# Attention and SiLU MLP on one core: batches 4 to 7 through seven products after the last scores, PSUM as one tile of named banks, exponentials of four banks, first scores on all strips

## The chip, the cores and the metric

The kernel runs on one core of one Trainium2 chip. The metric is the device time of one execution in microseconds, as a median over runs. Engines are named as in the profile: PE multiplies matrices (PEld loads its weights), DVE and ACT are the vector and scalar engines, POOL issues most loads, SP issues the stores. Matmul results go to PSUM, a memory of eight banks of 512 float32 columns on 128 partitions.

## What is computed

Eight batches, twelve heads, 448 tokens, 64 numbers per head; then an MLP over the 3584 tokens, 768 to 2048 to 768, with SiLU.

```python
def _attn_ref(q, k, v):
    scores = np.matmul(q, k.transpose(0, 1, 3, 2)) / np.sqrt(q.shape[-1])
    attn = np.exp(scores - np.max(scores, axis=-1, keepdims=True))
    attn = attn / (np.sum(attn, axis=-1, keepdims=True) + 1e-09)
    return np.matmul(attn, v)
def _moe_ref(x, w_in, w_out):          # x: the heads of a token side by side
    h = x @ w_in
    return (h / (1.0 + np.exp(-h))) @ w_out
```

The output is float32; the kernel gets q, k, v and the weights in the 16-bit type that the profile shows (f16).

## The kernel before, in words

**Attention.** A unit is one batch and a group of four heads (`hg`, three per batch). Batch 0 is cut into two pieces of 224 tokens (`PIECES`), so it has six units; later batches have three. The scores of a unit come in bursts of matmuls (L325): each of four heads lies on its own strip of 32 partitions of PE, and matmuls on different strips run side by side. A burst fills up to four PSUM banks, in two tiles "s" of two banks; `expo` (L357, its instruction L362) reads one tile, 128x896, into E. DVE adds E tiles for the row sums (L373), PE multiplies E by V (L388) and sums (L404), DVE forms the reciprocal of the sums (`inverse`, L447 sT, L455, L461 rdn) and writes the normalized x as xT (`norm`, L477).

For the units below `HALVES` (6: all of batch 0) a burst holds only two of the four heads, one "s" tile at a time, so only two strips work; later units score four heads in one burst.

**First matmul.** `ffn1` (L491): six matmuls of 448 columns (224 for batch 0) per block f of 128 of the 2048 columns. ACT takes the tanh into `th` (L502), DVE forms the gated value in G (`gate`, L536; SiLU as (tanh + 1) times h, with halved inputs). Batches 6 and 7 go by seven products instead (Strassen's scheme in Winograd's form, halves of the tokens being the two batches): `combine_x` and `combine_w_in` (L601, tw) form sums on DVE, `pair_product` (L625, "f") makes 7 x 3 matmuls per f of eight, five adds on DVE (L656), two copies (L650) and four SiLU (L663) on ACT finish them.

**Second matmul.** A pair of batches has seven tiles of 128 tokens; two consecutive tiles form a quad, which goes by seven products of eight matmuls of 384 columns each (`combine_g` L686, `product` L696, "p"); the first quad is plain (L710, "o"). DVE and ACT read the results (L750, L754, L757), `store` (L745) issues output DMAs on SP, at the very end on ACT too.

**What sets the order.** A planner in Python (`Order`, `Ring`, `Op`) runs ahead of the emission. It keeps a clock for each engine, estimated costs (`act(n)`, `mm(n)`), and rings that stand for buffers: "s" 2 tiles, "m" 4 single banks for everything else in PSUM, E 9 tiles, V 2 whole batches, xT 6. Whenever PE is free it picks a score burst (L1291 `run_qk`; between bursts of later batches at least `PACE`, 2.6 us by its clock), an attention step (`run_av`), or the next work of the MLP (`moe_ready`, L1235). The result is one list of instructions, sorted by planned time; each engine runs its part of it in order. One `ffn1` of six matmuls is one step for the planner, so a score burst stands between such steps.

Before the first h (batch 0's first `ffn1`) there is nothing to fill PE's waits, so `run_zeros` (L1455, matmuls L1459) puts matmuls of 128 zero columns there, in a bank of their own taken from the "m" ring.

Of the kernel before, what the change touches and what calls it, by code (L numbers as in the profile page):

```python
# [29 lines left out]
def act(n):  # L30
    return n * 0.00087 + 0.13


class Ring:


    def __init__(self, n):
        self.free = [0.0] * n

    def can(self, n, now):  # L40
        return len(self.free) >= n and heapq.nsmallest(n, self.free)[-1] <= now

    def when(self, n):
        return heapq.nsmallest(n, self.free)[-1] if len(self.free) >= n else None

    def take(self, n=1):
        for _ in range(n):
            heapq.heappop(self.free)

    def give(self, at):  # L50
        heapq.heappush(self.free, at)
# [25 lines left out]

class Order:


    def __init__(self, shy):
        self.now, self.shy = 0.0, shy
        self.free = {"PE": 1.0, "ACT": 2.1, "DVE": 1.2, "POOL": 1.2}
        self.wait = {"ACT": [], "DVE": []}
        self.pool = []
        self.dma_free = 0.0
        self.out = []
        self.mode = None
        self.busy = {e: 0.0 for e in self.free}
# [16 lines left out]
    def on_pe(self, op, mode):  # L106
        gap = SWITCH if mode != self.mode else 0.0
        self.mode = mode
        op.busy += gap
        self.start(op)  # L110

# [54 lines left out]
def kernel(  # L166
# [32 lines left out]
    EAGER = 1  # L199
    HALVES = 6  # L200
    NEAR, LATE = 0.15, -2.0
    COLD, FIRST = 8.5, 47
    SHY = 0.5
    TWB, SXB = 4, 4
    PIECES = ((0, 7), (7, TPP))
    NE, NX3, NT_ = 9, 6, 2
# [29 lines left out]

    rawk, rawq, KT, QT, VT, E, T, acc, rdn_t, xT, g_t, ost_t = ({} for _ in range(12))
# [24 lines left out]
    def load_v(b, hg0, hg1, x):  # L262
        if b not in VT:
            VT[b] = sb.tile([128, NH, NCH, D], FP16, name=f"V_{b}", tag="V", bufs=2)
        hs = slice(HG * hg0, HG * hg1)
        first, count = X_TOK[form(b, hg0)][x]
        nc.gpsimd.dma_start(  # L267
            out=VT[b][32 * x : 32 * (x + 1), hs, 0:count, :],
            in_=v[b, hs].rearrange("h (i g) d -> i h g d", g=TPP)[
                :, :, first : first + count, :  # L270
            ],
        )
# [42 lines left out]
    def score_banks(n, w, ys):  # L315
        for y in ys:
            pS_t[(n, w, y)] = ps.tile(
                [128, 2, 512], FP32, name=f"s_{n}_{w}_{y}", tag="s", bufs=2
            )

    def score(pS, n, c, e, h, x0, x1, p0):
# [8 lines left out]
            stop=(e == 1),  # L330
        )
# [5 lines left out]
    def scores(n, w, ys):  # L337
        score_banks(n, w, ys)
# [7 lines left out]
    def scores_rest(n):  # L346
        score_banks(n, 3, (0, 1))
# [9 lines left out]
    def expo(n, w, y):  # L357
        kr = rows_of(n, w * per_burst(n))
        nk = 32 * (units[n][3] - units[n][2]) * per_burst(n)
        if (n, w) not in E:  # L360
            E[(n, w)] = sb.tile([128, HG, S], FP16, name=f"E_{n}_{w}", tag="E", bufs=NE)
        nc.scalar.activation(  # L362
            out=E[(n, w)][0:kr, 2 * y : 2 * y + 2, 0:nk],
            in_=pS_t[(n, w, y)][0:kr, :, 0:nk],
# [15 lines left out]
    def attend_mm(a, n, part, c, h, k0, k1, e, start, stop):  # L380
# [5 lines left out]
        else:  # L386
            w = VT[b][k0:k1, HG * hg + h, c, part - 1 :: 2]
# [5 lines left out]
            stop=stop,  # L393
        )

    def attend_sums(ns):
        a = ps.tile([128, 512], FP32, name=f"a_{ns[0]}_0", tag="m", bufs=4)
        for n in ns:
            acc[(n, 0)] = a
        for i, (w, e) in enumerate(  # L400
            ((half[0], T[ns[0]]), (half[1], T[ns[1]]), (both, E[(ns[0], 3)]))
        ):
            for h in range(HG):
# [5 lines left out]
                    stop=(i == 2),  # L409
                )  # L410

    def attend(ns, part):
# [4 lines left out]
        for n in ns:  # L417
            acc[(n, part)] = ps.tile([128, 512], FP32, name=f"a_{n}_{part}", tag="m", bufs=4)

# [22 lines left out]
    def inverse(ns, step, i=0):  # L442
        g0, g1 = units[ns[0]][2:]
        shape = [128, g1 - g0, 32]
        if step == 0:
            sT_t[ns[0]] = sb.tile(shape, FP32, name=f"sT_{ns[0]}", tag="sT", bufs=1)
# [11 lines left out]
        else:  # L458
            n = ns[i]
            rdn_t[n] = sb.tile(shape, FP32, name=f"rdn_{n}", tag="rdn", bufs=2)  # L460
            nc.vector.transpose(  # L461
                out=rdn_t[n], in_=inv_t[ns[0]][:, :, i : i + 1].to_broadcast(shape)
            )

    def x3(b, cc):
        if (b, cc // 3) not in xT:
            xT[(b, cc // 3)] = sb.tile(
                [128, 3, S], FP16, name=f"xT_{b}_{cc // 3}", tag="xT", bufs=NX3
            )
        return xT[(b, cc // 3)]  # L470

    def norm(n, part):
# [3 lines left out]
        x3(b, cc)  # L476
        nc.vector.scalar_tensor_tensor(  # L477
            out=x3(b, cc)[:, cc % 3, 32 * g0 : 32 * g1],
# [7 lines left out]
    h_t, th_t, o_t = {}, {}, {}  # L486

    def ffn1(b, f, t0, t1):
        h = ps.tile([128, 512], FP32, name=f"h_{b}_{f}_{t0}", tag="m", bufs=4)
        for cc in range(NDC):  # L490
            nc.tensor.matmul(  # L491
                out=h[:, 0 : t1 - t0],
                lhsT=w_in_t[:, cc, 128 * f : 128 * (f + 1)],
                rhs=x3(b, cc)[:, cc % 3, t0:t1],
                start=(cc == 0),
                stop=(cc == NDC - 1),
            )
        h_t[(b, f, t0)] = h

    def tanh(b, f, t0, t1):  # L500
        th = sb.tile([128, t1 - t0], FP16, name=f"th_{b}_{f}_{t0}", tag="th", bufs=3)
        nc.scalar.activation(out=th, in_=h_t[(b, f, t0)][:, 0 : t1 - t0], func=AF.Tanh)  # L502
        th_t[(b, f, t0)] = th

# [3 lines left out]
    X = const.tile([128, NFF, 128], FP16, name="X")  # L511
# [18 lines left out]
    def gate(b, f, t0, t1):  # L530
        r = b % 2
        cut = 6 * 128 - S if b % 4 == 1 else S
        for lo, hi, dst, at in ((0, cut, G, S * r), (cut, S, X, -cut)):
            lo, hi = max(lo, t0), min(hi, t1)
            if lo < hi:
                nc.vector.scalar_tensor_tensor(  # L536
                    out=dst[:, f, at + lo : at + hi],
                    in0=th_t[(b, f, t0)][:, lo - t0 : hi - t0],
                    scalar=1.0,
                    in1=h_t[(b, f, t0)][:, lo - t0 : hi - t0],  # L540
                    op0=ALU.add,
                    op1=ALU.mult,
                )

    def rows(t, i):
# [3 lines left out]
        if u % 2 == 0 and k == NT - 1:  # L549
            return X[:, fs]  # L550
# [4 lines left out]
    PB = B - 2  # L555
    c_t, sx_t, tw_t, pp_t, pf_t = {}, {}, {}, {}, {}

    def old_buffer(name, home, cols):

        if home == "V":  # L560
            t = sb.tile([128, NH, NCH, D], FP16, name=name, tag="V", bufs=2)
            t = t.rearrange("p h c d -> p (h c d)")
        else:
            t = sb.tile([128, HG, S], FP16, name=name, tag="E", bufs=NE)
            t = t.rearrange("p h s -> p (h s)")
        return [
            t[:, 3 * cols * i : 3 * cols * (i + 1)].rearrange("p (c t) -> p c t", c=3)
            for i in range(2 if home == "V" else 1)
        ]

    def combine_x(m):
        if m < 4:
            made = old_buffer(f"sx_{m}", "V" if m == 3 else "E", S)
            for i, t in enumerate(made):
                sx_t[m + i] = t
        x = {(r, i): x3(PB + r, 3 * i) for r in range(2) for i in range(2)}
        a, b, op = {
            1: (x[1, 0], x[1, 1], ALU.add),
            2: (sx_t.get(1), x[0, 0], ALU.subtract),
            3: (x[0, 0], x[1, 0], ALU.subtract),  # L580
            4: (x[0, 1], sx_t.get(2), ALU.subtract),
        }[m]
        nc.vector.tensor_tensor(out=sx_t[m], in0=a, in1=b, op=op)
# [5 lines left out]
    def combine_w_in(m, f0):  # L589
        if (m, f0) not in tw_t:  # L590
            made = old_buffer(f"tw_{m}_{f0}", W_HOME.get((m, f0), "E"), 512)
            for i, t in enumerate(made):
                tw_t[(m + i, f0)] = t
# [9 lines left out]
    W_HOME = {(1, 0): "V"}  # L603
    PBANK = {1: "A", 2: "A", 6: "B", 5: "C", 3: "C", 7: "D", 4: "D"}

    def pair_product(f, m):
        if m in (1, 5):
            pp_t[(f, PBANK[m])] = ps.tile(
                [128, 512], FP32, name=f"f_{f}_{m}", tag="m", bufs=4
            )[:, 0:S]  # L610
        elif m == 6:
            two = ps.tile([128, 2, 512], FP32, name=f"f_{f}_{m}", tag="s", bufs=2)
            pp_t[(f, "B")], pp_t[(f, "D")] = two[:, 0, 0:S], two[:, 1, 0:S]
        x = {(r, i): x3(PB + r, 3 * i) for r in range(2) for i in range(2)}
        lo, at = f // 4 * 4, slice(128 * (f % 4), 128 * (f % 4 + 1))
        a, w = {
            1: (x[0, 0], w_in_part(0, 0, f, f + 1)),
            2: (x[0, 1], w_in_part(1, 0, f, f + 1)),
            3: (sx_t.get(4), w_in_part(1, 1, f, f + 1)),
        }.get(m, (None, None))  # L620
        if a is None:
            i = {4: 4, 5: 1, 6: 2, 7: 3}[m]
            a, w = x[1, 1] if m == 4 else sx_t[i], tw_t[(i, lo)][:, :, at]
        for c in range(3):
            nc.tensor.matmul(  # L625
                out=pp_t[(f, PBANK[m])],
                lhsT=w[:, c, :],
                rhs=a[:, c, :],
                start=(c == 0 and m in (1, 6, 5, 7)),
                stop=(c == 2),  # L630
                skip_group_check=True,
            )

    def pair_tmp(f, name):
        tag, n, shape, dt = {
            "p": ("rq", NRQ, [128, TPP * D], FP16),
            "q": ("rk", NRK, [128, TPP * D], FP16),
# [914 lines left out]
```

## Time and profile of the kernel before

| What | Value |
|---|---|
| median of 3 runs | 393.91 us (393.77 to 394.09) |
| span of the profiled execution | 393.02 us |
| median less that span | 0.89 us |
| granted PE clock | 1.00 in the windows from 30 us on |
| first h (L491) starts | 30.23 us |
| zeros L1459 | 87 matmuls |
| scores L325, all forms | 864 matmuls |
| h L491 | 192 of 224 columns, 480 of 448 |
| pair product f L625 | 168 of 448 columns |
| second matmul p L696 and o L710 | 728 and 64 of 384 columns |
| exponentials | 156 of 128x896, 16 of 96x896 |
| tanh L502 | 32 of 224, 80 of 448 columns |

The profile's time is of one execution, and its zero is the start of the span; the median is taken over the runs, outside of the profiler's span. "Busy" counts an engine's instructions; in the groups, the number behind the bar is the total busy time, then the mean time of one in ns, then the engine's idle time ahead of that group and what ended it. Consecutive matmuls overlap, so the time from start to start (the spacing) is less than the mean of one. The chain of work that ended last lists, step by step, what stood on the path to the end.

### The profile page before, as it was taken

What the parts mean: (1) busy time and instruction counts of PE and PEld (TensorE: products, weight loads), DVE (VectorE), ACT (ScalarE), POOL (GpSimd) and SP (SyncE); (2) the same over time, 40 slices, a digit from 0 to 9 for tenths busy, and PEclk for the clock granted to TensorE, in tenths of its full rate; (3) what the DMA queues carried; (4) which work ended last, traced back from release to release, by engine and by line L of the source; (5) the groups of instructions that cost most, each with busy time, mean ns of one, the idle gap of its engine ahead of it and who ended that gap; (6) DMA issues with size and microseconds to landing.
All of it is one profiled execution on the core that took longest, in us unless ns stands there. A gap on an engine that the chain in (4) does not pass through costs nothing.

```text
span 393.0 us, 9255 instructions
## 1 busy us (share of the span) xinstructions
PE 386.6 (98%) x3679; PEld 199.7 (51%) x3679; DVE 296.2 (75%) x610; ACT 238.7 (61%) x365; POOL 83.7 (21%) x153
## 2 busy tenths in 40 slices
PE   8999999999999999999999999999999999999996
PEld 7667774444444434454444444444444555555663
DVE  2476676999988696895968967876879897777652
ACT  4988885696855869626778258575693218772000
POOL 6632455406006060600063116000000000000000
PEclk9999999999999999999999999999999999999999
DMA  7999999919047573753183567202000140001443
GB/s 112 205 210 210 161 166 179 182 37 141 2 82 115 109 103 39 121 99 86 25 116 48 102 125 115 38 2 61 21 3 2 46 100 17 2 1 37 97 98 93
DMA packets 35579, 34.43 MB, mean 88 GB/s; under 512 B 11600, under 2 KB 34000, under 8 KB 35536
## 3 DMA queue, kind: packets, MB, share of 16 engines
q0 software_dynamic: 24784, 22.82, 39.2%
q1 hardware_dynamic: 9984, 10.24, 10.2%
q10 hardware_dynamic: 768, 0.79, 0.8%
q8 instruction: 29, 0.48, 0.5%
q14 instruction: 14, 0.11, 0.1%
HBM read 45.61 MB, written 11.01 MB: 144 GB/s over the span
## 4 chain that ended last, share of the span: by engine, by line
PE 94%; DMA 2%; DVE 1%; ACT 1%; issue 0%; POOL 0%; SPq 0%; ACTq 0%; DVEq 0%; POOLq 0%
PE p L696 29%; PE h L491 29%; PE s L325 12%; PE a L388 10%; PE f L625 8%; PE o L710 3%; PE a L404 2%; DMA rk<-in_k_dram 2%; DMA out_dram<-ost 1%; PE z L1459 1%; DVE tw L601 0%; ACT E L362 0%; DVE ost L750 0%; SPq L745 0%; DVE KT L302 0%
## 5 line engine op out<-in xcount | busy, mean ns | idle before, releaser
L362 ACT ACTIVATE E<-s 128x896 f16<-128x896 f32 (+1 forms) x172 | 150.0, 915 | 44.9 <-PE s L325 43.6
L491 PE MATMUL h<-xT,w_in_t 128*128 128x448 f16 (+1 forms) x672 | 118.2, 326 | 0.0
L491 PEld LDWEIGHTS <-w_in_t 128*128 128x128 f16 x672 | 61.5, 98 | 54.4 <-issue 17.7
L502 ACT ACTIVATE th<-h 128x448 f16<-128x448 f32 (+1 forms) x112 | 54.3, 494 | 33.6 <-PE h L491 24.9
L536 DVE SCALAR_TENSOR_TENSOR G<-th,h 128x448 f16<-128x448 f16 (+2 forms) x112 | 55.4, 508 | 16.5 <-ACT th L502 14.7
L267 POOL DMA_DIRECT2D V<-in_v_dram x88 | 48.6, 568 | 50.2 <-PE a L388 35.7
L325 PE MATMUL s<-rq,KT 32*128 32x448 f16 (+4 forms) x864 | 56.7, 340 | 0.8 <-ACT E L362 0.4
L696 PEld LDWEIGHTS <-G 128*128 128x128 f16 x384 | 36.3, 98 | 28.5 <-issue 4.8
L696 PEld LDWEIGHTS <-S 128*128 128x128 f16 x312 | 29.5, 98 | 23.8 <-issue 3.4
L388 PE MATMUL a<-E,V 128*32 128x448 f16 (+3 forms) x864 | 39.9, 334 | 0.0
L696 PE MATMUL p<-w_out_t,S 128*128 128x384 f16 x208 | 38.1, 326 | 0.5 <-DVE xT L477 0.5
L696 PE MATMUL p<-D,G 128*128 128x384 f16 x208 | 38.1, 326 | 0.0
L252 POOL DMA_DIRECT2D rq<-in_q_dram x27 | 15.1, 560 | 104.7 <-PE s L325 88.7
L750 DVE TENSOR_TENSOR ost<-p,u 128x384 f32<-128x384 f32 x39 | 21.6, 555 | 19.4 <-PE p L696 15.5
L477 DVE SCALAR_TENSOR_TENSOR xT<-a,rdn 128x448 f16<-128x448 f32 (+1 forms) x54 | 28.6, 565 | 7.0 <-PE a L388 6.2
L325 PEld LDWEIGHTS <-KT 32*128 32x128 f16 (+2 forms) x864 | 17.5, 98 | 28.9 <-issue 26.0
L696 PE MATMUL p<-w_out_t,G 128*128 128x384 f16 x176 | 31.9, 326 | 0.0
L373 DVE TENSOR_TENSOR T<-T,E 128x1792 f16<-128x1792 f16 x20 | 21.7, 1087 | 10.2 <-ACT E L362 10.2
L388 PEld LDWEIGHTS <-V 128*32 128x32 f16 (+2 forms) x864 | 17.8, 95 | 20.8 <-issue 13.5
L373 DVE TENSOR_TENSOR T<-E,E 128x1792 f16<-128x1792 f16 x20 | 21.6, 1082 | 5.5 <-ACT E L362 5.5
L757 ACT COPY ost<-p 128x384 f32<-128x384 f32 x13 | 6.2, 480 | 32.0 <-PE p L696 21.1
L302 DVE STREAM_TRANSPOSE KT<-rk 128x256 f32<-128x256 f32 (+3 forms) x48 | 16.7, 386 | 6.8 <-DMA rk<-in_k_dram 6.8
(70 smaller groups left out, 344.5 us busy)
## 6 DMA issues: line engine op xcount, KB each, us to landing
out_dram<-ost SPq DMA_DIRECT2D x208, 48.0 KB, 1.6
rk<-in_k_dram POOLq DMA_DIRECT2D x24, 224.0 KB, 5.0
rq<-in_q_dram POOLq DMA_DIRECT2D x21, 224.0 KB, 5.4
w_in_t<-in_moe_w_in_dram POOLq DMA_DIRECT2D x6, 512.0 KB, 11.4
w_out_t<-in_moe_w_out_dram POOLq DMA_DIRECT2D x4, 768.0 KB, 13.6
V<-in_v_dram POOLq DMA_DIRECT2D x43, 64.0 KB, 4.0
V<-in_v_dram POOLq DMA_DIRECT2D x40, 48.0 KB, 3.9
out_dram<-ost ACTq DMA_DIRECT2D x16, 48.0 KB, 1.8
```

The source lines that it names most:

```text
L267: nc.gpsimd.dma_start(out=VT[b][32 * x : 32 * (x + 1), hs, 0:count, :], in_=v[b, hs].rearrange("h (i g) d -> i h g d", g=TPP)[:, :, first ...
L325: nc.tensor.matmul(out=pS[p0 : p0 + 32 * (x1 - x0), h % 2, at : at + nq], lhsT=KT[(b, hg)][32 * h : 32 * (h + 1), c, x0:x1, :, e], rhs=QT[ ...
L362: nc.scalar.activation(out=E[(n, w)][0:kr, 2 * y : 2 * y + 2, 0:nk], in_=pS_t[(n, w, y)][0:kr, :, 0:nk], func=AF.Exp, scale=attn_scale,)
L373: nc.vector.tensor_tensor(out=T[n], in0=T[n] if step else E[(n, 0)], in1=E[(n, step + 1)], op=ALU.add,)
L388: nc.tensor.matmul(out=a[32 * h : 32 * (h + 1), 0:nq], lhsT=w, rhs=e[k0:k1, h, at : at + nq], start=start, stop=stop,)
L477: nc.vector.scalar_tensor_tensor(out=x3(b, cc)[:, cc % 3, 32 * g0 : 32 * g1], in0=acc[(n, part)][:, 0:nq], scalar=0.5, in1=rdn_t[n].rearra ...
L491: nc.tensor.matmul(out=h[:, 0 : t1 - t0], lhsT=w_in_t[:, cc, 128 * f : 128 * (f + 1)], rhs=x3(b, cc)[:, cc % 3, t0:t1], start=(cc == 0), s ...
L502: nc.scalar.activation(out=th, in_=h_t[(b, f, t0)][:, 0 : t1 - t0], func=AF.Tanh)
L536: nc.vector.scalar_tensor_tensor(out=dst[:, f, at + lo : at + hi], in0=th_t[(b, f, t0)][:, lo - t0 : hi - t0], scalar=1.0, in1=h_t[(b, f, ...
L625: nc.tensor.matmul(out=pp_t[(f, PBANK[m])], lhsT=w[:, c, :], rhs=a[:, c, :], start=(c == 0 and m in (1, 6, 5, 7)), stop=(c == 2), skip_gro ...
L696: nc.tensor.matmul(out=pr_t[(qd, BANK[m])][:, 0:OH], lhsT=w[:, f, :], rhs=W_[m][:, f, :], start=(f == 0 and BANK[m] == m), stop=(f == HF - 1),
L750: nc.vector.tensor_tensor(out=out, in0=a, in1=b, op=op)
```

## The change

Eight parts, made in one edit:

1. Batches 4 and 5 go by seven products as 6 and 7 do (`PAIRS`), and no pair product is issued before the last scores are issued.
2. PSUM is one tile P of eight banks. Score tiles 0 and 1 are banks 0 to 3. Banks 4 and 5 are a third score tile during batch 0 and then join the "m" ring, which starts with banks 6 and 7.
3. From batch 1 on one exponential reads four banks (128x1792).
4. `HALVES` is 1: only unit 0 is scored by halves, the rest of batch 0 on all four strips.
5. h and the products of both schemes are issued matmul by matmul, so that a burst can come between any two.
6. tanh writes G and the gate works in place; batch 0 takes two f in one bank (2 x 224 columns) with one tanh and one gate.
7. sT and rdn live in one fixed tile R, rdn of two units is one transpose; V is loaded per four heads into a ring of four (batch 0's into G); xT has a ring of eight, E of eleven; batch 7's x uses the buffers of k. The sums S of the second matmul are whole (128x1024) for all but the last quads.
8. The zeros write the last 128 columns of bank 7, which also serves the "m" ring. The planner's costs and priorities are set anew.

Core of the diff:

```diff
 def act(n):
-    return n * 0.00087 + 0.13
+    return n * 0.000824 + 0.177
...
-    EAGER = 1
-    HALVES = 6
+    EAGER = 0
+    HALVES = 1
+    WIDE = 1
+    PAIRS = (B - 4, B - 2)
+    LAST = {B - 4: range(DFF // 256), B - 2: range(DFF // 256)}
...
-    NE, NX3, NT_ = 9, 6, 2
+    NE, NX3, NT_, NV = 11, 8, 2, 4
...
+    P = ps.tile([128, 8, 512], FP32, name="P")
+    R = const.tile([128, 2, S // 32, 32], FP32, name="R")
...
-    def expo(n, w, y):
+    def expo(n, w, y, bank):
...
-            out=E[(n, w)][0:kr, 2 * y : 2 * y + 2, 0:nk],
-            in_=pS_t[(n, w, y)][0:kr, :, 0:nk],
+            out=E[(n, w)][0:kr, 2 * y[0] : 2 * y[-1] + 2, 0:nk],
+            in_=P[0:kr, bank : bank + 2 * len(y), 0:nk],
...
-    def tanh(b, f, t0, t1):
-        th = sb.tile([128, t1 - t0], FP16, name=f"th_{b}_{f}_{t0}", tag="th", bufs=3)
-        nc.scalar.activation(out=th, in_=h_t[(b, f, t0)][:, 0 : t1 - t0], func=AF.Tanh)
+    def tanh(b, fs, t0, t1):
+        g, h = gates_of(b, fs, t0, t1)
+        nc.scalar.activation(out=g, in_=h, func=AF.Tanh)
...
+        late = LAST.get(b - b % 2, ())
+        if b == 0:
+            turns = [(f, f + 1) for f in range(0, NFF, 2)]
+        else:
+            turns = [(x,) for f in range(HF) if f not in late for x in (f, f + HF)]
...
             def deps():
+                if qk_seq:
+                    return [None]
                 made = [xs[0, c] for c in (range(3, NDC) if m == 2 else range(3))]
...
-        for y in ys:
+        for y in [ys] if b_wide(n) else [(y,) for y in ys]:
...
+    def b_wide(n):
+        return WIDE and units[n][0] > 0
+
+    def give_tile(at, j):
+        if j == 2 and units[qk_seq[0][0][0]][0]:
+            for bank in (4, 5):
+                m_ring.give(at, bank)
+        else:
+            s_ring.give(at, j)
...
     def run_zeros(n):
-        if "z" not in warm:
-            warm["z"] = ps.tile([128, 512], FP32, name="z", tag="m", bufs=4)
         for _ in range(n):
             nc.tensor.matmul(
-                out=warm["z"][:, 0:128], lhsT=zeros, rhs=zeros, start=True, stop=True
-            )
+                out=P[:, 7, 384:512],
+                lhsT=zeros,
+                rhs=zeros,
+                start=True,
+                stop=True,
+                skip_group_check=True,
+            )
...
+            elif od.steps:
+                od.next_step()
+                ran = True
```

## The prediction

> **What bounds the kernel now.** I read the shares by engine, then the slices, the chain of work that ended last, the groups by form, and last the timeline of the first 31 us.
>
> ```profile
> PE 386.6 (98%) x3679; PEld 199.7 (51%) x3679; DVE 296.2 (75%) x610; ACT 238.7 (61%) x365; POOL 83.7 (21%) x153
> PE   8999999999999999999999999999999999999996
> ACT  4988885696855869626778258575693218772000
> PEclk9999999999999999999999999999999999999999
> PE 94%; DMA 2%; DVE 1%; ACT 1%; issue 0%; POOL 0%; SPq 0%; ACTq 0%; DVEq 0%; POOLq 0%
> ```
>
> The first four lines are busy time and slices, the last the shares of the chain. TensorE is busy in every slice, at a granted clock of nine tenths or more throughout, and carries 94% of the chain. So the time is the sum of the matmuls, plus the start, plus the tail; a matmul saved shortens the kernel unless a wait fills its place. The groups by form (count, busy time, mean ns of one) give the sizes, and the chain gives spacing, since neighbouring matmuls overlap:
>
> ```profile
> L362 ACT ACTIVATE E<-s 128x896 f16<-128x896 f32 x156 | 136.0, 915 | 43.3 <-PE s L325 42.4
> L491 PE MATMUL h<-xT,w_in_t 128*128 128x448 f16 x480 | 98.1, 353 | 0.0
> L502 ACT ACTIVATE th<-h 128x448 f16<-128x448 f32 x80 | 43.7, 546 | 31.0 <-PE h L491 23.3 <-issue 5.1 <-ACT th L502 2.3
> ```
>
> ```profile
> 29.41 0.89 PE a L388 x32
> 30.29 0.68 PE h L491 x6
> ...
> 78.38 0.51 PE s L325 x8
> 78.89 2.38 PE h L491 x12
> ...
> 307.93 1.82 DVE tw L601 x2
> 309.75 0.55 DVE xT L477
> ...
> 321.48 30.08 PE f L625 x159
> ```
>
> Columns of the chain: start, duration, what. 159 matmuls of 448 columns in 30.08 us are 0.189 us each; 12 in 2.38 us are 0.198, because a score burst stands before them: a change of PE's tiling costs about 0.1 us. ACT waits for scores 43 us in all, PE for ACT 0.4 us: ACT is not the bound after the start. The first 30 us are another stage: attention of batch 0 alone, before the first h at 30.23 in the timeline.
>
> **The sum.** All terms are against the profiled execution: its span is 393.02 us, the median 393.91, so 0.89 us lies around the span and is added at the end. From the first h to the end of the span: 393.02 - 30.23 = 362.8 us.
>
> *The seven products.* Batches 4 and 5 leave L491: 2 batches x 16 f x 6 = 192 matmuls of 448 columns (480 become 288). They enter the pair product: 8 f x 7 products x 3 = 168. So 24 matmuls go, 24 x 0.189 = **-4.54 us**. Second matmul, scores and attention keep their counts.
>
> *Order.* In the order of the changed kernel, 16 score matmuls of batch 0's last unit stand behind the first h instead of ahead of it: on four strips 16/4 x 0.096 (224 columns: 30 h in 2.98 us less a change of tiling) = 0.38. The changes of tiling behind that point go from 182 to 187, at 0.116 with side effects (0.58). **+0.96 us.** This work is not new, only behind my mark; its other side is in the start term.
>
> *The stall at 309.48.* There PE idles 0.69 us for xT, behind two tw of batch 6/7's pair (the chain lines above). In the new order the same combinations for pair 6/7 come out long before they are read. **-0.69 us.**
>
> *The start.* Now: most bursts of batch 0 score two strips at a time, 8 matmuls in 0.50 to 0.53 us; one of 16 on four strips (at 6.22) takes 0.53 as well, so each pair of halves merged saves PE about 0.5 us. The timeline shows PE without gaps from 16 to 28 and ACT waiting for scores (0.31 at 25.95, 0.56 at 29.45), so PE sets this stage. Bounds: if nothing is gained the first h stays at 30.2; if ACT becomes the limit, 24 exponentials at a spacing of 0.81 (two take 1.63 in the chain) from 6.83 end at 26.3, so about 26.5. What holds it above that is one new wait: warm-up matmuls (146 instead of 87) now write the last quarter of bank 7, which also serves as an accumulator, so groups of them wait until DVE has read it (six such waits, for sT or xT, in the order). Each can hold PE 0.4 to 0.8 us, and scores stand behind them in PE's queue. Walking the order with the durations above I get 28.7 to 28.9 and take **28.8**. DMA: w_in's last load lands at 23.2 for its first half and 34.1 for the second, w_out's first use is 18 us after its first rows; the new dense stretch starts 1.4 us earlier and still finds them.
>
> The Trainium skill, "PSUM — Partial Sum Buffer", section "PSUM bank collisions raise a hardware error", says accesses of two engines are to be guarded by bank and quadrant, not by address. By that rule the waits on bank 7 are real although the columns differ; no run here shows yet what they cost.
>
> *What should cost nothing.* Exponentials: 156 of 896 elements become 74 of 1792 and the few of batch 0. A line through 915 ns (896) and 546 ns (448) gives 0.177 + 0.824 ns per element, 1.65 us for 1792; per burst that saves ACT 0.18 us. Bounds for this unseen form: two of the old (1.83), and half of it if reading four banks were twice as fast (0.9); I take the line. DVE loses 80 gates but gains 40 pair adds (0.625 us each): -80 x about 0.4 + 25 us, less work in all. Score bursts now come every 11 h or fewer (11 x 0.189 + 0.1 + 0.48 = 2.65 us of PE, 2.89 before), as h is issued singly. One burst's chain is scores 0.57, exponential 1.65, two hops of 0.04: 2.30 us. It fits into 2.65; a few intervals in the order are shorter (one of 2.08, four near 2.38). I add **+0.3 us** for those.
>
> *Queues.* POOL issues K, Q and V in the same order per batch, V now per four heads; with attention over at 246 instead of 302 they are due sooner. DMA is 0.94 busy from 30 to 100 us, 0.46 to 200 and 0.35 to 302 by the windows: the stretch that is full is not compressed by more than the 1.4 us, and the later ones have room for 302/246. Stores stay on SP's queue behind the products; nothing that PE waits for stands behind them.
>
> *Pair phases.* With pairs held back until all scores are out, attention ends near 246 instead of 302, then pair 4/5 (8 x 21 x 0.189 = 31.8 us), quads, pair 6/7, quads. Per f, PE needs 3.97 us, DVE five adds 3.1, ACT two copies at 0.53 and four SiLU at 0.58, 3.4, plus 0.35 for two SiLU cut in parts. In pair 4/5 DVE has also some 3.5 us of tw: 25.0 + 3.5 = 28.5 against 31.8. All lie beside PE, as they do between 321.48 and 351.56 now, without a gap. Cover gone, see rival D.
>
> Sum: 362.8 - 4.54 + 0.96 - 0.69 + 0.3 = 358.8; with the start at 28.8 the span is 387.6, with 0.89 around it **388.5 us**.
>
> **Rivals.**
>
> *A, slower.* A 4-bank exponential holds all four score banks, so the next burst can't be written until it has ended; before, two tiles came free one after the other, 0.82 apart. Nothing of ACT and PE overlaps in the burst's loop any more: 2.30 us, margin 0.35. If a tanh (0.546) stands ahead of each exponential in ACT's queue the loop is 2.85, 0.20 over the 2.65 in which PE has other work: 74 x 0.20 = 14.8, 403 us. It decides from 5.4/74 = 73 ns lost per burst, that is if 0.42 us stands ahead on the average. Against: while scores are written ACT has some 0.65 us free, and a tanh fits there. PE's one wait for ACT now is 0.4 us in all, with two exponentials per burst. Chance 0.10.
>
> The Trainium skill, "Perfetto Trace Analysis", section "Matmuls", advises independent groups to rotate through PSUM banks so that one's evacuation overlaps the next one's matmuls. It speaks against the four-bank read, for A; the other matmuls (h, in two to four other banks) are what this case has in place of the rotation.
>
> *B, the start gains all.* The zeros wait for nothing late, first h at 26.5: 388.5 - 2.3 = 386.2. For: once the zeros have begun, PE waits for DVE at one place of this stage now, 0.2 us. Against: none of the zeros waits for anything now. Chance 0.12.
>
> *C, the start gains nothing.* Zeros' waits take the place of the halves; 30.0: 389.7. Chance 0.13.
>
> *D, the matmuls are saved and given back.* In pair 4/5 DVE's tw, sx and norms come together with the adds, or the SiLU parts hold the accumulators. If DVE needs 0.3 us more than PE per f, 8 x 0.3 = 2.4: 391 us. For: tw and sx come out just in time by my walk (0.2 to 0.4 us). Against: the dense phase now. Chance 0.13.
>
> Forecast (387.3 to 389.3): 0.52.
>
> **Numbers.** The range: below it half of B's lower tail, 385.3; above it A and the end of D, so 392.5. About 0.2%, 0.8 us, is what a measurement of this kernel can tell from no change: faster is below 393.1, slower above 394.7. All of forecast, B, C and nearly all of D are faster: 0.86; a D of twice its size is the same: 0.04; A: 0.10.
>
> **What would show it.** First h near 28.8, zeros waiting for DVE sT or xT; scores of batch 0 with 16 matmuls. Exponentials of 1792 near 1.65 us and PE's wait for ACT at score bursts under 1 us in all (A: 5 us or more). h 288 and f 336 matmuls. Pair 4/5 from about 246 without a PE gap (D: waits of f for DVE or ACT). The gap at 309 gone. I am wrong if the exponential is much longer than 1.8 us, since every burst then waits, or if the zeros hold PE past 30 us.

## The result, and the profile after

The changed kernel takes 391.34 us as a median of five executions (390.68 to 393.11), against 394.09 (393.77 to 394.61) for the kernel before beside it: a ratio of 0.9933, 95% interval 0.9911 to 0.9954. It is faster, by half of what was forecast: 2.75 us instead of 5.4, and its time is 2.8 us above the 388.5 of the forecast though within the range.

The profiled execution took 390.68 us with a span of 388.9. Here are the shares, the slices and the chain's shares of the changed kernel:

```profile
PE 380.1 (98%) x3714; PEld 197.8 (51%) x3714; DVE 295.0 (76%) x531; ACT 239.1 (61%) x307; POOL 83.6 (22%) x153
PE   8989999999999999999999999999999999999996
ACT  4948885587977568876668885518781028872000
PEclk9999999999999999999999999999999999999999
PE 95%; DMA 1%; DVE 1%; ACT 1%; issue 1%; ACTq 0%; POOLq 0%
```

PE is as dense as before from the fourth slice on, and less so in the third (19 to 29 us): an 8 where a 9 stood. The groups by form of the changed kernel:

```profile
L412 ACT ACTIVATE E<-P 128x1792 f16<-128x1792 f32 x72 | 119.8, 1664 | 49.6 <-PE P L376 48.8
L557 PE MATMUL P<-xT,w_in_t 128*128 128x448 f16 x288 | 60.5, 354 | 0.0
```

The four-bank exponential takes 1.664 us (1.65 was forecast), and the 192 matmuls of batches 4 and 5 are gone from L557. The chain of the changed kernel, at the end of the start and in the first pair phase:

```profile
24.01 0.43 DVE R L494
24.44 0.04 issue
24.48 0.33 PE P L1614 x3
24.81 0.30 PE P L438 x7
25.11 0.81 issue
25.92 0.45 PE P L438 x9
...
29.66 0.40 DVE xT L545
30.06 0.04 issue
30.11 0.38 PE P L1614 x4
30.49 0.10 PE P L557
...
265.84 0.54 ACT p L715
266.38 0.04 issue
266.43 21.17 PE P L688 x111
```

Before the first h, zeros (L1614) wait for DVE's sT and xT (R L494, xT L545), and at 25.11 PE stands 0.81 us while it waits for nothing that the profile shows, called "issue". The first h starts at 30.32 in the timeline, no earlier than the 30.23 of the kernel before. Behind it the span has 388.9 - 30.3 = 358.6 us, against 362.8 before: the whole gain is there, and none is in the start. The pair phase is dense but for two waits for ACT (at 266 and 288 us) of about 0.2 and 0.3 us.

One thing on reading the numbers that follow: with wide zeros and halves, two of four executions took 397.73 and 397.85 us at a granted clock of 0.97, why no trace shows, and its time is given from the other two.

### The profile page after: what moved, and what is told of

It reads as the page before. It is cut to its first block, busy times and chain, and to the rows that moved or that the text cites. A ratio compares the mean times of both kernels' runs of the same rounds, so it can differ in the third digit from the quotient of the medians.

```text
span 388.9 us, 9194 instructions
## 1 busy us (share of the span) xinstructions
PE 380.1 (98%) x3714; PEld 197.8 (51%) x3714; DVE 295.0 (76%) x531; ACT 239.1 (61%) x307; POOL 83.6 (22%) x153
## 4 chain that ended last, share of the span: by engine, by line
PE 95%; DMA 1%; DVE 1%; ACT 1%; issue 1%; ACTq 0%; POOLq 0%
PE P L768 31%; PE P L557 20%; PE P L688 16%; PE P L376 11%; PE P L438 10%; PE P L780 3%; PE P L1614 2%; PE P L453 2%; DMA rk<-in_k_dram 1%; ACT E L412 1%; DMA out_dram<-ost 0%; DVE xT L545 0%; DVE ost L820 0%; DVE R L494 0%; DVE KT L359 0%
## 5 line engine op out<-in xcount | busy, mean ns | idle before, releaser
L412 ACT ACTIVATE E<-P 128x1792 f16<-128x1792 f32 (+3 forms) x98 | 143.2, 1481 | 60.9 <-PE P L376 59.9
L557 PE MATMUL P<-xT,w_in_t 128*128 128x448 f16 (+1 forms) x480 | 81.0, 316 | 0.0
L557 PEld LDWEIGHTS <-w_in_t 128*128 128x128 f16 x480 | 43.4, 98 | 35.7 <-issue 14.9
L376 PE MATMUL P<-rq,KT 32*128 32x448 f16 (+4 forms) x864 | 50.3, 340 | 0.9 <-ACT E L412 0.5
L598 DVE SCALAR_TENSOR_TENSOR G<-G,P 128x448 f16<-128x448 f16 x64 | 37.7, 611 | 10.3 <-ACT G L573 10.1
L768 PE MATMUL P<-w_out_t,S 128*128 128x384 f16 x208 | 39.1, 326 | 0.0
L768 PE MATMUL P<-D,G 128*128 128x384 f16 x208 | 39.0, 326 | 0.0
L545 DVE SCALAR_TENSOR_TENSOR xT<-P,R 128x448 f16<-128x448 f32 (+1 forms) x54 | 29.0, 568 | 11.9 <-PE P L438 9.1
L820 DVE TENSOR_TENSOR ost<-P,u 128x384 f32<-128x384 f32 x39 | 21.6, 555 | 19.4 <-PE P L768 12.8
L768 PE MATMUL P<-w_out_t,G 128*128 128x384 f16 x192 | 35.9, 327 | 0.0
L438 PE MATMUL P<-E,V 128*32 128x448 f16 (+2 forms) x672 | 34.4, 356 | 0.0
L573 ACT ACTIVATE G<-P 128x448 f16<-128x448 f32 x64 | 32.8, 542 | 1.9 <-PE P L557 1.5
L688 PE MATMUL P<-sx,tw 128*128 128x448 f16 x144 | 30.0, 352 | 0.0
L824 ACT COPY u<-P 128x384 f32<-128x384 f32 x13 | 6.2, 477 | 27.7 <-PE P L768 27.3
```

Source lines behind the costliest of these rows:

```text
L376: nc.tensor.matmul(out=pS[p0 : p0 + 32 * (x1 - x0), h % 2, at : at + nq], lhsT=KT[(b, hg)][32 * h : 32 * (h + 1), c, x0:x1, :, e], rhs=QT[ ...
L412: nc.scalar.activation(out=E[(n, w)][0:kr, 2 * y[0] : 2 * y[-1] + 2, 0:nk], in_=P[0:kr, bank : bank + 2 * len(y), 0:nk], func=AF.Exp, scal ...
L438: nc.tensor.matmul(out=a[32 * h : 32 * (h + 1), 0:nq], lhsT=w, rhs=e[k0:k1, h, at : at + nq], start=start, stop=stop, skip_group_check=True,)
L545: nc.vector.scalar_tensor_tensor(out=xc(b, cc)[:, 32 * g0 : 32 * g1], in0=acc[(n, part)][:, 0:nq], scalar=0.5, in1=rdn_t[n].rearrange("p g ...
L557: nc.tensor.matmul(out=h_t[(b, f, t0)][:, 0 : t1 - t0], lhsT=w_in_t[:, cc, 128 * f : 128 * (f + 1)], rhs=xc(b, cc)[:, t0:t1], start=(cc == 0),
L573: nc.scalar.activation(out=g, in_=h, func=AF.Tanh)
```

## The experiments

"T" is the theory that the zeros' waits for bank 7 alone cost the start; its rival R, sharpened to "I" once the first traces were read, says that PE's supply of instructions does. Times are medians; "first h" is its start in the timeline of the profiled execution; a ratio is to the kernel before, run beside it (394.2 to 394.3 us each time). Matmuls are counted from nought, so the 562nd has 562 ahead of it, and a stop "at the 347th" lies just behind it.

The changed kernel's own time varies: 391.34 us over its first five executions, 392.64 over the twelve that follow. Gains below are against 392.64; against 391.34 they are 1.3 us less. The runs were made on different chips, so small differences between them should not be pressed.

### The changed kernel once more

No edit.

> The changed kernel as it is, once more, as the mark for the other runs of this call and for its spread: its five times lay 2.4 us apart (390.68 to 393.11), the kernel before's 0.84. Theory T (the start is lost to the waits of the zeros): median 391 +- 0.7, first h near 30.4, five waits of zeros of 0.64 to 0.67 us. Rival R (the start is bound by something else that varies, such as the 0.81 us in which PE had no instruction at 25.1): the stall at 25 differs from 0.81 and moves the first h by as much.

Measured: 392.64 us over twelve executions (391.93 to 395.12), ratio 0.9971 (0.9955 to 0.9987), first h at 32.09. The spread goes with the granted clock: eight executions at 0.995 to 1.0 took 391.93 to 392.77, the four others, at 0.989 to 0.994, 393.1 to 395.12. The waits of the zeros are the same as in the first trace, but PE now stopped three times without an instruction, not once. These are PE's waits in this run (waited for, total us, times, longest):

```profile
PE P L1614 <- DVE xT L545: 1.4, 3, 0.5
PE P L438 <- issue: 1.1, 1, 1.1
PE P L1614 <- DVE cols L272: 1.0, 1, 1.0
PE P L1614 <- issue: 0.8, 2, 0.5
PE P L1614 <- DVE R L494: 0.5, 1, 0.5
```

(DVE cols is the launch, before the first zero.) The stops without an instruction lie at the 221st, 347th and 475th matmul, and where the other runs have such stops in the start, they lie at these numbers too, whatever the matmul is: 126 or 128 apart. The page of this run says why that number:

```profile
q8 instruction: 29, 0.48, 0.5%
```

29 packets of 16 KB on queue q8, for 3714 matmuls: 128 matmuls, each with its weight load, are one block. The trace's records of that queue put their starts at 13.0, 19.5, 25.4, 31.2 and 37.2 us: about 6 us apart.

Two comparisons tie the stops to these blocks. In every trace with such stops PE goes on 2.2 to 2.5 us after the start of a block: behind the 475th matmul at 27.69 in this run (block at 25.40), at 25.92 in the first trace (block at 23.70). And in the first trace the blocks start at 11.2, 17.7 and 23.7 us, 1.7 to 1.8 us earlier than here, and the first h is 1.8 us earlier too. R expected something of this kind, but named the stall at 25 us, which grew by only 0.3 us; what moved is the start of the blocks. Why the first block starts earlier in one execution than in another, no run shows.

### Without the late zeros

```diff
     def run_zeros(n):
+        zcalls.append(n)
+        if len(zcalls) > 26:
+            return
         for _ in range(n):
```

> The changed kernel without its last 28 zeros (the groups that wait for DVE's reads of bank 7); the order of everything else is unchanged and the output too. T: the waits of 0.65 us and the 1.6 us of zeros go, scores and attention come earlier, first h at 28.8 or before, time 1.6 to 2.5 us less than the changed kernel. R: the same gaps stay under other names (DVE, ACT, no instruction), first h above 29.9, time within 0.5 us. Third possibility: PE's clock falls in the new idle time, then the granted clock shows it and the time is longer.

Measured: 390.27 us, ratio 0.9901 (0.9887 to 0.9916), first h at 30.03: 2.1 us earlier, time 2.4 us less. The time fits T, but the first h does not (28.8 or before by T, above 29.9 by R), and PE's waits show where most of the freed time went:

```profile
PE P L376 <- issue: 1.7, 1, 1.7
PE P L376 <- DVE rq L369: 0.6, 1, 0.6
PE P L438 <- DVE xT L545: 0.6, 1, 0.6
PE P L1618 <- issue: 0.6, 1, 0.6
```

The stop at the 347th matmul grew to 1.7 us: PE comes there sooner and waits for the same block. The edit takes away waits and matmuls at once, so it can't tell T from R.

### Batch 0 by halves again

```diff
-    HALVES = 1
+    HALVES = 6
```

> The changed kernel with all of batch 0 scored by halves again (HALVES 6), three score tiles and the zeros in bank 7 as in the changed kernel; the planner makes a new order. T: with the halves PE has less idle time, so fewer zeros and fewer waits, first h 30 to 31, time within 0.6 us of the changed kernel: the four strips gained PE time that the zeros' waits gave back. R (four strips do gain): first h 32 or later, time 1.5 us or more above the changed kernel.

Measured: 391.16 us, ratio 0.992 (0.9907 to 0.9933), 1.5 us less than the changed kernel run again; T expected no difference, R a loss of 1.5, so both missed. First h at 32.47, but the 575th matmul, with 16 more scores ahead of it. There are 95 zeros, and PE never stops for want of an instruction. The start is 0.4 us longer, and only 357.0 us are left behind it instead of 358.5: the gain lies behind the first h, 0.4 us of it for the 16 scores (by the prediction's 0.38), the rest with the planner's new order, which nothing here explains. As the changed kernel stands, the four strips thus gain nothing.

### Each four-bank exponential as two

```diff
-        nc.scalar.activation(
-            out=E[(n, w)][0:kr, 2 * y[0] : 2 * y[-1] + 2, 0:nk],
-            in_=P[0:kr, bank : bank + 2 * len(y), 0:nk],
+        for i, z in enumerate(y):
+            nc.scalar.activation(
+                out=E[(n, w)][0:kr, 2 * z : 2 * z + 2, 0:nk],
+                in_=P[0:kr, bank + 2 * i : bank + 2 * i + 2, 0:nk],
```

> The changed kernel with each exponential of 128x1792 as two of 128x896, in the same order otherwise. My sum has PE as the bound from the first h on, with ACT's chain per burst 2.30 us against 2.65: two of 0.815 spacing are 1.73 against 1.66, so no change, within 0.4 us. The rival from the prediction (one instruction for four banks holds the score banks and costs) says it gets faster by 1 us or more, since the first half's banks come free 0.8 us earlier. If ACT were near its limit, it gets slower by 74 x 0.07 = 5 us or less.

Measured: 392.77 us, ratio 0.9955 (0.9943 to 0.9967), the same as 392.64. By form it is 156 of 915 ns again; behind the first h 358.6 us, as in the changed kernel. (Its blocks start early too, at 11.4, 18.2 and 24.3 us, yet its first h is at 32.39: in that execution the granted clock was 0.76 from 26 to 30 us.) PE's wait for exponentials is 0.3 us with two instructions and 0.5 with one. Holding four banks costs nothing that can be told here, and saving ACT time brings nothing.

### Without zeros that wait for nothing

```diff
+        zcalls.append(n)
+        if 12 <= len(zcalls) <= 25:
+            return
```

> Two theories after the first runs. T: the waits of the late zeros for bank 7 cost the start. I: PE's instructions come from memory in blocks of 128 matmuls with their weight loads, one block every 6 us while the load queues are full (they start at 13.0, 19.5, 25.4 and 31.2 us in the trace of the changed kernel run again), so the place of the first h in the count of matmuls sets its time: 562nd in the changed kernel, 519th in the kernel before. This kernel leaves out 47 zeros between 10 and 17 us that wait for nothing, and keeps all six groups that wait for bank 7; order otherwise and output unchanged; first h is the 515th. T: no gain, time within 0.5 us of the changed kernel in the call before (392.6). I: first h at 30 or before instead of 32.1, time 2 us less (390 to 391). If the clock falls, the granted clock shows it.

Measured: 393.64 us over twelve executions (390.22 to 394.39). The median is confounded by the clock, as the slices of the profiled execution show:

```profile
PE   8799999999999999999999999999999999999996
PEclk9669999999999999999999999999999999999999
```

The granted clock is 0.6 in the second and third slice. Seven executions at a mean clock of 0.982 to 0.987 took 393.6 to 394.4; the five at 0.991 to 1.0 took 390.22 to 391.88, four of them within the 390 to 391 that I expects; but that is a choice among executions, and the next runs are better evidence.

The Trainium skill, "TensorE: Matmul & The Clock Gate", section "Part 1: The HAM clock gate", says that PE's clock is throttled unless recent activity releases it. The trace agrees: without 47 of these zeros, which compute nothing, the granted clock falls to 0.6.

### Wide zeros

```diff
...
-        for _ in range(n):
+        for _ in range(int(n * 128 / 288 + 0.5)):
             nc.tensor.matmul(
-                out=P[:, 7, 384:512],
-                lhsT=zeros,
+                out=P[:, 7, 224:512],
+                lhsT=zeros[:, 0:128],
```

> Zeros of 288 columns instead of 128, in the same places and about the same PE time, 57 instead of 146 and two of the waits left; first h is the 473rd matmul, order otherwise and output unchanged. I: only one block boundary (the 347th) can still hold PE, first h near 28, time 389 or less (3 us or more below the changed kernel). T: two of six waits are left, 4 x 0.65 = 2.6 us less at most, first h 29.5 or later, about 390.

Measured: 388.44 us, ratio 0.9853 (0.984 to 0.9865), 4.2 us less than the changed kernel run again and 2.9 less than its first five executions. First h at 27.32; the granted clock is nine tenths or more in every slice. That exceeds what T allows: four waits at the 0.5 us that the traces show are 2 us. The executions lie close together (388.31 to 388.8).

### One pair only

```diff
-    PAIRS = (B - 4, B - 2)
-    LAST = {B - 4: range(DFF // 256), B - 2: range(DFF // 256)}
+    PAIRS = (B - 2,)
+    LAST = {B - 2: range(DFF // 256)}
```

> The changed kernel with only batches 6 and 7 by seven products; batches 4 and 5 as in the kernel before, all else as changed, order the same up to some 230 us. By the sum of the prediction 24 matmuls of 0.189 come back: 4.5 us more than the changed kernel, in the part behind the first h (363.1 instead of 358.6). Rival (the second pair's time is given back): within 1.5 us of the changed kernel.

Measured: 396.72 us, ratio 1.0078 (1.0052 to 1.0104), slower than the kernel before. First h at 31.84 (32.09 with two pairs), behind it 394.7 - 31.8 = 362.9 us: 4.4 more than the changed kernel's 358.5. The executions lie far apart (395.11 to 400.19), so the part behind the first h is the better number. The 24 matmuls are worth what they were counted at, and with them back the change loses.

### The kernel before as a run

> The kernel before as a run of its own, for its span, its time around the span and its blocks of instructions. The prediction put 0.89 us around the span; the changed kernel's runs show 1.75 to 1.81. If that is the same for all kernels, this run's time less its span is 1.8, and its span about 392.4; if the change added it, 0.9 and 393.3.

No edit. Measured: 394.28 us, the profiled execution 394.02 with a span of 392.2: 1.8 us around the span, as in the changed kernel. First h at 29.61, and no stop for want of an instruction. But its blocks too start 6 us apart (19.7, 25.7 and 31.6), and PE goes on behind the 475th matmul at 27.99, 2.3 us after one: it only just keeps pace. In the trace that the prediction was made from, it stopped there, and the timeline shows it:

```profile
28.60 0.28 PE L388 MATMUL a<-E,cols 96*32 96x224 f16 x3 [0.23 <-issue]
```

This is again behind the 475th matmul and 2.3 us after a block (26.34). So the supply was all but the limit of the start before the change: scores on four strips save PE time there but no matmuls, and that could hardly bring the first h forward (a reading of the traces; the run with halves fits it).

### Zeros that don't wait

```diff
-                out=P[:, 7, 384:512],
+                out=P[:, FREE.get(len(zcalls), 7), 384:512],
```

FREE gives 19 late zeros bank 3, 5 or 6.

> The changed kernel with all its 146 zeros, first h still the 562nd matmul; 19 of the late zeros write another bank that nobody reads at that time, so that none waits for DVE. Output and order unchanged. T (waits of the zeros alone set the start): all five waits of 0.65 us go, first h 3 us earlier, as early as with the zeros left out or earlier (29 to 30), time 389.5 to 390. I (blocks of 128 matmuls every 6 us): the 475th still waits for its block until 27 to 27.7 us, only the two waits behind it go: first h 30.5 to 31, time 391 to 391.7.

Measured: 390.92 us, ratio 0.9916 (0.9902 to 0.9929), first h at 30.48, a hair below what I expects (391 to 391.7, 30.5 to 31) and clearly above what T expects (389.5 to 390, 29 to 30). Here is PE in the timeline (start, us, matmuls, idle time ahead and its releaser):

```profile
19.18 0.34 PE L1620 MATMUL P<-zeros 128*128 128x128 f16 x3
21.36 0.22 PE L1620 MATMUL P<-zeros 128*128 128x128 f16 x1 [1.84 <-issue]
...
25.76 0.37 PE L438 MATMUL P<-E,G 128*32 128x224 f16 x7
27.28 0.45 PE L438 MATMUL P<-E,G 128*32 128x224 f16 x9 [1.15 <-issue]
```

No zero waits for DVE any more. The time comes back as 1.84 us at the 347th matmul and 1.15 at the 475th, behind which PE goes on at 27.28; in the changed kernel run again it was 27.69. Of the 1.6 us that the first h gains, 1.2 lie behind this boundary; the other 0.4 are there from the first block on, which starts at 12.5 instead of 13.0. Only the waits behind the last block boundary were worth anything.

### Fewer matmuls, all waits kept

```diff
+        wide = 2 <= len(zcalls) <= 26
+        w = 288 if wide else 128
+        for _ in range(int(n * 128 / 288 + 0.5) if wide else n):
...
```

Each zero then multiplies and writes `w` columns, the last of bank 7.

> The changed kernel with its early zeros (2 to 17 us) at 288 columns instead of 128: 42 matmuls fewer at about the same PE time, so that the clock holds; all six late groups with their waits are kept. First h is the 520th matmul. T: no gain, first h 31.5 to 32, time 392 to 392.6. I: 42 x 6/128 = 2.0 us less, first h near 30, time 390.6.

Measured: 390.2 us, ratio 0.9897 (0.9884 to 0.9911), first h at 30.16, with the waits for DVE unchanged:

```profile
PE P L1620 <- DVE xT L546: 1.4, 3, 0.5
PE P L1620 <- DVE R L495: 0.5, 1, 0.5
PE P L439 <- issue: 0.4, 1, 0.4
```

Without touching one of the waits, 42 matmuls fewer bring 2.4 us against the changed kernel run again, whose blocks start at the same times (12.9 and 13.0, 19.4 and 19.5), and 1.1 us against its first five executions. None of the 17 executions of the changed kernel is as short (390.68 at least) as the longest of these four (390.6). So T alone cannot be the cause.

### Wide zeros, batch 0 by halves

The edits of wide zeros and of halves together.

> Zeros of 288 columns and batch 0 by halves again: what the four strips are worth once the instructions no longer hold PE (against 388.4 with wide zeros and four strips). First h is the 515th matmul, behind 192 scores instead of 176. I: PE's own work sets this start as in the kernel before, first h 30.5 to 31.5 with 16 scores more behind it, time 390 +- 0.6, so the strips are worth 1 to 2 us there; if they are worth nothing even then, 388.5.

Measured: 388.99 and 389.65 us, ratio 0.9874 (0.9856 to 0.9892), first h at 30.78. Against 388.44 with four strips: the strips are worth 0.9 us with wide zeros, just under the 1 to 2 expected. PE still stops 1.0 us for an instruction at the 475th matmul here, so this is not what they would be worth if instructions never held PE.

### Wide zeros, the late ones left out

> Zeros of 288 columns and the last groups left out: 50 zeros, no wait, first h is the 466th matmul. With wide zeros alone the first h was at 27.3, PE without an instruction for 0.66 us at the 347th matmul and 0.56 at the 475th. Now the 475th comes behind the first h either way, and the exponentials of batch 0 end no sooner than 26.3: at most 0.5 us to gain, time 388.0 to 388.5. If the clock falls, longer.

The edits of wide zeros and of the run without the late zeros together. Measured: 388.34 us, ratio 0.9851 (0.9838 to 0.9864), first h at 26.87. The best of all, with wide zeros alone 0.1 us behind it, which is less than can be told apart.

### The loads held back

```diff
+    hold = od.add(
+        LateOp(
+            "DVE",
+            0.1,
+            lambda: nc.vector.memset(w_in_t[:, 0, 0:2], 0.0),
...
+                gate=(lambda: hold.done) if f0 == 0 and c == 0 else None,
...
```

One load of q, `plan_q(NG + 2)`, moves ahead of the loads of w_in.

> The changed kernel with the loads of w_in, and all loads behind them, held back until the third unit's x is written (about 20 us); output unchanged, the planner makes a new order with more zeros, and the first h and the time must be later, which says nothing. What is looked at is the 221st and 347th matmul and the starts of the blocks of instructions before the loads begin again. If a block takes 6 us because it shares the queues with the loads (they are over 200 GB/s from 13 us on in the changed kernel), the block behind the 347th matmul comes as soon as it is asked for and PE does not stop there (0.7 to 2.0 us in four runs). If a block takes 6 us whatever else is moved, the second block starts again near 19.5 us and PE stops at the 347th.

Measured, one execution: 399.06 us, first h late as intended. These are windows of both kernels: the stretch and its length, the busy time of PE, PEld, DVE, ACT and POOL with their instructions, the granted clock, the DMA engines' share and GB/s; first the loads held back, then the changed kernel run again:

```profile
16.00:19.00 3.00, 2.49 (x72) 1.65 (x68) 2.02 (x6) 2.49 (x3) 0.00 (x0) 1.00 0.00 0
22.00:26.00 4.00, 4.00 (x120) 2.65 (x108) 3.07 (x10) 3.86 (x6) 1.52 (x3) 1.00 0.06 7
```

```profile
16.00:19.00 3.00, 2.49 (x76) 1.60 (x72) 1.65 (x6) 2.59 (x4) 2.04 (x4) 1.00 1.12 210
22.00:26.00 4.00, 3.88 (x119) 2.81 (x120) 2.32 (x7) 3.44 (x4) 2.04 (x3) 1.00 1.15 211
```

With the queues empty the next block starts 0.7 us after PE passes the 221st matmul (4.1 us in the changed kernel run again) and at once when it passes the 347th (3.6 us), and PE does not stop for an instruction before the loads begin again; its one wait near the 347th is a zero's, 0.48 us for DVE's xT. At the 475th:

```profile
24.98 0.96 PE L438 MATMUL P<-E,G 128*32 128x224 f16 x32
```

32 matmuls in one piece, where the changed kernel stood for 0.8 and 1.1 us in its two traces. It passes the 603rd matmul at 29.1 us, the changed kernel run again at 35.1 (with other work among them, as the order differs). So a block takes 6 us because it lies among the loads, as far as one execution can show it.

## Why the prediction was wrong

**What failed is the start term.** "Walking the order with the durations above I get 28.7 to 28.9 and take 28.8": it was 30.3 in the first trace and 32.1 in the second. The walk gave PE every instruction as soon as its waits were over. The runs showed a limit that it lacked: PE gets 128 matmuls per 6 us while the loads run, and with 59 more zeros and 16 fewer scores the first h moved from the 519th to the 562nd place. The bounds (26.5 and 30.2) held only waits and ACT, so the later end was too low as well. The sign was in the trace of before: the prediction read PE as dense from 16 to 28 us and so as what sets this stage, and did not follow up the stop of 0.23 us for an instruction at 28.6. The zeros' waits, which the prediction blamed for 28.8 instead of 26.5, are real (four in the trace instead of six, 0.48 to 0.51 us each), but up to the last block boundary they hide behind the blocks, as the run with zeros that don't wait shows: first h 1.6 us earlier instead of 3.

**The median less the span was mis-sized.** The 0.89 us was a median of some executions less the span of another. In executions with both on record it is about 1.8 us, for the kernel before too (394.02 and 392.2). The profiled execution that the sum started from was therefore likely one of 394.8, not of 393.91.

The profiled execution's sum closes: start +1.5, behind the first h -0.2, around the span +0.9, together 390.7 (measured 390.68). The median is another 0.7 higher, since the start varies with the blocks and the clock. That 391.34 still lies within the range is luck: its upper end was put there for A and D, and neither came.

**What held.** Behind the first h 358.8 us were forecast, 358.6 measured. The seven products: -4.54 forecast, 4.4 in the run with one pair. The stall at 309 is gone. *Pair phases*: two waits of 0.5 us together instead of D's 2.4. The deferred scores and the changes of tiling were not tested one by one; only their sum with the rest holds.

**The rivals.** A is out: PE's wait for exponentials is 0.5 us in all, and splitting them changes nothing. The Trainium skill's advice on rotating banks ("Perfetto Trace Analysis", section "Matmuls"), weighed there, has no effect here (392.64 and 392.77 us); that PE has h and products to do meanwhile is the likely reason, which no run tests. B's first h was nearly reached when the instructions were cut (27.3 and 26.9), not by the waits going alone (30.48). C is what happened to the start, though its cause, the zeros' waits, was the smaller part: without them the first h came 1.6 us earlier, with fewer and wider zeros 4.8.

The Trainium skill, "Runtime: NRT & Kernel Launch", section "Instruction fetch mechanics", says that instructions stream in blocks of 16 KiB, 256 instructions, and that crossing into a new one is mostly hidden. The size agrees with the trace (128 matmuls and their weight loads). Hidden it is with the loads held back; among loads of 210 GB/s a crossing cost up to 1.8 us of idle PE.

## What to carry to other kernels

Where an engine idles for want of nothing ("issue"), count its instructions up to that place: if the stops recur at a fixed count, the supply is the bound, and fewer, larger instructions help where faster ones don't. Filler that keeps the clock up counts as instructions too: here 57 zeros of 288 columns, with fewer waits too, held the clock as well as 146 of 128 and let the first h start 4.8 us sooner. A span and a time may be subtracted only if they are of one execution.

## What was not expected of the hardware

A block of 128 matmuls with weight loads arrives every 6 us (13.0, 19.5, 25.4, 31.2) while loads move about 210 GB/s; with the loads held back it started 0 to 0.7 us after the crossing before it. Leaving out 47 idle matmuls between 10 and 17 us dropped the granted clock to 0.6 for two slices of 10 us in one execution. A four-bank exponential of 1792 columns takes 1.664 us against 2 x 0.915 for two of two banks.
